# Dealing the stages of an RWKV-7 and feed-forward kernel so that each slot of a unit uses one TensorE tile mode

## The chip, the cores and the metric

The kernel runs on one core of one Trainium2 chip. The metric is the device time of the core in microseconds. Every number of a profile comes from one profiled execution of the program, whose own time is named beside its span.

## The reference

Two blocks, one after the other. The first is the RWKV-7 recurrence over batch 4, 8 heads, 768 steps, head dimension 40, in float32:

```
for t in range(S):
    y[:, :, t] = einsum('bhd,bhde->bhe', r_t, state)
    Sa = einsum('bhde,bhe->bhd', state, a_t)
    state = state * w_t[:, :, None, :] - einsum('bhd,bhe->bhde', Sa, b_t)
    state = state + einsum('bhd,bhe->bhde', v_t, k_t)
x = y.transpose(0, 2, 1, 3).reshape(B * S, H * D)      # 3072 tokens x 320
h = x @ w_in                                           # 320 -> 2048
out = (h * clip(h + 3, 0, 6) / 6) @ w_out              # 2048 -> 320
```

The two weight matrices come in double precision and the kernel converts them itself, early in the run.

## The kernel before

**Units.** The sequence is cut into 12 blocks of 64 steps. A unit is one block of two of the four batch entries, with all heads, so that its 2 x 64 rows fill the 128 partitions. There are 24 units, numbered 0 to 23, four to a group; unit 8 is the ninth. Units i and i+2 share a state tile, so the recurrence runs from unit i to unit i+2. Each unit goes through stages, each of which is a few TensorE instructions and then the evacuation of their result from PSUM by VectorE (DVE), ScalarE (ACT) or GpSimd (POOL):

- ahead of its turn (function `prepare`): W turned (transposed) and scanned into running products (`w_stage`, L584 and L604), gam and rgam made from them (`gam_stage`, second scan L615, copies L632 to L639), A, B and K turned and multiplied with them (L652, L660, L747), `factor` (rgam turned, copied to `rgt` at L722, and K and B scaled by it on POOL at L733 into `KBt`), F (64x64 products, four ACT copies L694 and L697, the matrix to be inverted), E (products, masked on DVE at L565) and EV (products, L766).
- in its turn (function `step`): RT and VT (R and V turned, L907 and L940), S (the state turned, L952 and L957), R (L929, L933), U (L979, L983), UT (L1022, L1028), C (products L539 in `scores`, masked on DVE at L565; then POOL copies V beside it at L1006 and SP fetches a later V at L470), rS (L1039, copied at L1045), H (L539, masked at L565), ysn (64 products L1082; its results go through DVE L1089 and POOL L1090 into `yg`, and into the state at L1094), and move and move2, eight DMAs of `yg` into the feed-forward input `xt` (L1130, L1135).

Every four units, a group's F is inverted by some 60 small DVE operations in turn (L812, L818; `invert`, in a list called `side`), and the first two units of the next group each carry a block of two small products (`third_block`, L848 and L872) that complete the inverse `tinv`, which U reads.

**Tile modes.** The page writes a matmul's stationary operand as rows*columns. The feed-forward products are 128*128. Turns from unit 8 on are 64*128 or 40*128 (two row halves, all columns). The recurrence's products are 64*64 or 40*64 (halves in both directions). I call these the full, the turn and the product mode.

**Slots and gaps.** From unit 8 on (the loop at the end of the kernel) each unit has five slots. A slot first issues the TensorE part of all its stages, and then all evacuations, in the order of the list `AFTER`. What a slot's stages write to PSUM lies in two tiles named `pair` of two banks each, of which there are two in all; the list `FILLS` says which stages share one. After each slot comes a gap of feed-forward pieces: 2.7 of them (2.2 in units 8 and 9; 3.6 while an inversion is in `side`, whose DVE steps are then laid between the pieces). A feed-forward job is half of a unit's hidden features, in eight pieces: four of `expand` (called e1 to e4; 8 instructions of 128x128 at L1186 each) and four of `contract` for the job before (L1227). A job also has 16 short 64*128 products on the third part of `xt` (`short`, kept in the list `narrow`). They are in the turn mode. Each slot begins by issuing them if they are waiting; otherwise they come out ahead of the third piece of `contract`. The first job of a unit can start once `xt` has landed.

The slots in the code, where the first number is the distance of the unit meant:

```
SLOTS = [
    [(0, "RT VT"), (-1, "U UT")],
    [(0, "S R"), (3, "EV"), (4, "E")],
    [(5, "A B"), (-1, "H")],
    [(6, "W"), (-1, "ysn"), (0, "C"), (6, "gam")],
    [(-1, "move move2"), (5, "K factor F"), (0, "rS")],
]
```

SP issues nearly all DMAs, in program order. In slots 3 and 4 its order is: W, V (after the POOL copy L1006), the eight of move and move2 (after `yg`), B and K of the next unit (after POOL's L733). Slot 0 adds R, slot 2 adds A, and the output rows (L1251) come after a unit's last contraction.

Of the kernel before, what the change touches and what calls it, by code (L numbers as in the profile page):

```python
# [12 lines left out]
ALU = mybir.AluOpType  # L13
# [5 lines left out]
BL = 64  # L19
# [12 lines left out]
def kernel(  # L32
# [42 lines left out]
    nc = tc.nc  # L75
# [373 lines left out]
    def fetch(name, i, engine=None):  # L449

        if i is None or i >= NK:
            return
        x, crossed = {"W": (w, 0), "A": (a, 0), "B": (b, 0), "K": (k, 0), "R": (r, 1),
                      "V": (v, 1)}[name]
        if name == "V":
            t = values[i % AHEAD if i < 2 * NU + AHEAD else (i - 2 * NU - 2) % NU]
        else:
            t = placed.get((name, i))
            if (name, i) == ("R", 1):
                t = others["K"]  # L460
            t = t if t is not None else (others if i < 2 * NU and i % 2 and name != "R" else inputs)[name]
        g, p = names[i]
        engines = engine or nc.sync
        for q in range(2):
            engine = engines[q] if isinstance(engines, tuple) else engines
            y = x[2 * p + q, :, g * BL:(g + 1) * BL, :]
            rows = slice(q * BL, (q + 1) * BL)
            if crossed:
                for s in range(2):
                    engine.dma_start(out=t[rows, 4 * s:4 * s + 4, 0:D],  # L470
                                     in_=y[s::2].rearrange("h t e -> t h e"))
# [57 lines left out]
    def half(i, n=SLOT):  # L529
        return slice(SLOT * i, SLOT * i + n)  # L530

    def scores(lhs, rhs, swap=False, placed=False):


        o = every_other(1) if placed else ps_pair(NPR, BL)
        for n in range(NPR):
            for q in range(2):
                for i in range(2):
                    nc.tensor.matmul(out=o[i][half(q), n ^ (2 * q * placed), :],  # L539
                                     lhsT=lhs[half(i, D), n ^ (2 * q * swap), half(q)],  # L540
                                     rhs=rhs[half(i, D), n, half(q)], start=True, stop=True)
        return o
# [26 lines left out]
    def prepare(i, F):  # L569
# [39 lines left out]
        def gam_stage():  # L609
# [5 lines left out]
            nc.vector.tensor_tensor_scan(out=back, data0=back, data1=start[:], initial=0.0,  # L615
                                         op0=ALU.mult, op1=ALU.add)
            nc.vector.memset(first, 1.0)
            if late and i % (NU + 3) == 0:
                gam = _ap(homes["prods1"][:], 0, [[P, NPR], [1, P]])
            else:  # L620
                gam = grp.tile([P, NPR, P], F32, name="gam", tag="gam", bufs=NU + 2)
# [84 lines left out]
        def factor_stage():  # L706

            if halves:
                wide = D if late else SLOT
                rg = ps_pair(NPR, wide)  # L710
                for pr in range(NPR):
                    for s in range(2):
                        nc.tensor.transpose(out=rg[s][:, pr, :], in_=o["rg"][half(s, wide), pr, :],
                                            identity=ident[half(s, wide), half(s, wide)])
            else:
                rg = ps_any([P, NPR, P])
                for pr in range(NPR):
                    nc.tensor.transpose(out=rg[:, pr, :], in_=o["rg"][:, pr, :], identity=ident[:])
            yield PE
            rgt = tmp.tile([P, H, D], F32, name="rgt", bufs=RGT)  # L720
            if halves:
                nc.scalar.activation(out=rgt[:].rearrange("p (r s) e -> p s r e", s=2), in_=rg[2][:, :, :, 0:D],  # L722
                                     func=AF.Copy)
            else:
                nc.scalar.activation(
                    out=rgt[:], in_=rg[:].rearrange("p r (s e) -> p (r s) e", s=2)[:, :, 0:D],
                    func=AF.Copy,
                )
            t = grp.tile([P, HD + WPAD], F32, name="KBt", tag="KBt", bufs=NU + 2)
            nc.gpsimd.memset(t[:, 2 * HD:], 0.0)  # L730
            for x, name in enumerate("KB"):
                o[name] = t[:, x * HD:x * HD + WPAD]
                nc.gpsimd.tensor_tensor(  # L733
                    out=o[name][:, 0:HD].rearrange("p (h e) -> p h e", h=H),
                    in0=o[name + "N"][:, :, 0:D], in1=rgt[:], op=ALU.mult,
                )
# [17 lines left out]
        def ev_stage():  # L754
# [10 lines left out]
            for x in range(2):  # L765
# [2 lines left out]
            o["EV"] = EV  # L768

        return {"W": w_stage, "gam": gam_stage, "A": a_stage, "B": b_stage, "F": f_by_32 if i < 2 * NU else f_by_64,  # L770
                "factor": factor_stage, "K": k_stage, "E": e_stage, "EV": ev_stage}

    def in_turn(stages, order):

# [118 lines left out]
    def step(i):  # L893
# [8 lines left out]
        def s_RT():  # L902
# [6 lines left out]
                fetch("R", i + 1)  # L909
            if fresh:  # L910
                nc.gpsimd.tensor_copy(last_dec[p][:], dec[:, 1])
                return
            scale = tmp.tile([P, 2, NPR], F32, name="scale", bufs=2)
            nc.gpsimd.tensor_tensor(out=scale[:], in0=last_dec[p][:], in1=dec[:, 0], op=ALU.mult)
            nc.gpsimd.tensor_copy(last_dec[p][:], dec[:, 1])
# [81 lines left out]
                                 func=AF.Copy, scale=-1.0)  # L997

        def s_C():
            x = scores(m["VT"], m["RT"])  # L1000
            yield PE
            if i < 2 * NU:
                m["K"] = masked(x)
                return
            masked(x, beside["K"][:, :, 0:BL])
            nc.gpsimd.tensor_copy(beside["K"][:, :, BL:JOIN].rearrange("p (r x) d -> p r x d", r=2),  # L1006
                                  VN[:].rearrange("p (x r) d -> p r x d", r=2)[:, :, :, 0:D])
            if i > 2 * NU:
                fetch("V", i + NU)

        def s_UT():

# [17 lines left out]

        def s_rS():

            ysp = [x.rearrange(("p (j q) t -> p j q t", "p r (j q) t -> p r j q t")[n // 2], q=2)
                   for n, x in enumerate(every_other(1))] if i >= 2 * NU else ps_pair(2, 2, BL)
            for j in range(2):
                for q in range(2):
                    for s in range(2):
# [7 lines left out]
            nc.scalar.activation(out=ys[:].rearrange("p (j r) q t -> p r j q t", r=2), in_=ysp[2], func=AF.Copy)  # L1045

        def s_sn():
            wide = SLOT if i < NU else D
# [84 lines left out]
        def s_move2():  # L1133
            for dst, src in m["moves"][4:]:
# [1 line left out]
            ready[i] = m["xt"]  # L1136
            yield from ()

        return {"RT": s_RT, "R": s_R, "VT": s_VT, "S": s_S, "U": s_U, "C": s_C, "UT": s_UT,
                "rS": s_rS,  # L1140
                "sn": s_sn, "ysn": s_ysn, "H": s_H, "y": s_y, "move": s_move, "move2": s_move2}

# [413 lines left out]


    SLOTS = [
        [(0, "RT VT"), (-1, "U UT")],
        [(0, "S R"), (3, "EV"), (4, "E")],  # L1560
        [(5, "A B"), (-1, "H")],
        [(6, "W"), (-1, "ysn"), (0, "C"), (6, "gam")],
        [(-1, "move move2"), (5, "K factor F"), (0, "rS")],
    ]
    FIRST_SLOTS = {
        (0, 0): [(0, "RT VT"), (5, "W"), (-1, "y"), (5, "gam")],
        (0, 1): [(-1, "move move2"), (0, "S R"), (4, "EV")],
        (0, 2): [(5, "A B")],
        (0, 3): [(6, "W"), (0, "C"), (6, "gam")],
        (0, 4): [(5, "K factor F"), (0, "rS")],  # L1570
        (1, 1): [(0, "S R"), (4, "E")],
    }
    FILLS = ["RT VT".split(), "U UT".split(), "S R EV".split(), ["E"], "A B".split(), ["H"],
             ["ysn"], "W C y".split(), "K factor".split(), "F rS".split()]
    AFTER = "U UT RT VT S EV R E H A B y ysn W C gam move move2 K factor F rS".split()
# [23 lines left out]
    def slot(i, j):  # L1599

        afresh()
        begun, taken = [], {}
        if narrow:
            narrow[0]()
        if j == 0 and i < NK:
            units[i] = step(i)
        for k, names_ in FIRST_SLOTS.get((i - 2 * NU, j), SLOTS[j]):
            u = i + k
            if u >= NK:
                continue  # L1610
            for name in names_.split():
                if k > 0 and u < 2 * NU + AHEAD and name != "EV":
                    continue
                if name == "W":
                    comings[u] = prepared(u)
                rest = (comings if k > 0 else units)[u][name]()
# [16 lines left out]

    begun_homes()
    begun_fixed()
    pairs.clear()
# [12 lines left out]
    while jobs or next(stream):  # L1649
        next(stream)  # L1650
# [30 lines left out]
```

## Time and profile before

| | |
|---|---|
| three runs | 818.2, 818.77, 815.56 us (median 818.2) |
| the profiled execution | 818.15 us, of which 816.4 us are the span from its first to its last instruction |
| PE (matmul) busy | 735.3 us, 90% of the span |
| PE weight loads | 617.7 us, 76% |
| DVE / ACT / POOL busy | 492.5 / 318.9 / 171.9 us |
| mean granted TensorE clock | 0.955 |
| the loop from unit 8 on | R turned for unit 8 at 312.9 us; last ysn at about 767 us |
| after the loop | feed-forward products alone, to about 805 us |

Of the page, the second part (40 slices of 20.4 us) shows PE at 9 tenths from the seventh slice on, and DVE between 2 and 8 tenths, high where an inversion runs. In the windows of the loop, DVE is busy for 26.0 of 29.0 us between 512 and 541 us (an inversion runs) and for 6.6 of 21.0 us between 711 and 732 us (none runs). A row of the timeline reads: start, duration, engine, line, operation, output and inputs, shape of the stationary operand (rows*columns), shape of the moving one, count. The ends of matmuls are modelled and overlap their successors, so what TensorE spends is read from start to start.

### The profile page before, as it was taken

Reading aid. Unit: us, or ns where it says so; the run is one execution under the profiler, and the core shown is the slowest. Engines: PE = TensorE matmul, PEld = TensorE weight load, DVE = VectorE, ACT = ScalarE, POOL = GpSimd, SP = SyncE. Lnnn points to the kernel's source line nnn. Section 1 sums busy time; section 2 is a strip of 40 time slices with the busy share of each in tenths; the row PEclk is TensorE's granted clock in tenths of the full one; section 3 lists DMA queues with packets and bytes.
Section 4 is the critical chain, followed back from the end, with each engine's and each line's share of the span. In section 5 each row is a group of like instructions: output and inputs, shape, how many; then the busy total and the mean of one; then the engine's idle time right before and its main releaser. Section 6 shows DMA issues by size and latency. Waiting matters only on the chain.

```text
span 816.4 us, 33518 instructions
## 1 busy us (share of the span) xinstructions
PE 735.3 (90%) x14960; PEld 617.7 (76%) x14960; DVE 492.5 (60%) x967; ACT 318.9 (39%) x646; POOL 171.9 (21%) x322
## 2 busy tenths in 40 slices
PE   5626768999999989999989999999999999999998
PEld 4626756878778877778778778878788887888886
DVE  7896786599545798445777355878344863232210
ACT  3348981323445333442333552333452234322121
POOL 6403002321222304222121222122022102110000
PEclk9855898999999999999989999999999999999999
DMA  9683554311233303231231222221211111100000
GB/s 122 119 188 104 140 134 76 67 27 26 54 63 58 67 20 58 49 62 29 54 58 29 45 44 50 55 54 35 51 41 31 21 35 29 25 15 19 20 9 17
DMA packets 174207, 44.91 MB, mean 55 GB/s; under 512 B 157424, under 2 KB 172784, under 8 KB 174064
## 3 DMA queue, kind: packets, MB, share of 16 engines
q1 hardware_dynamic: 169760, 42.03, 26.5%
q8 instruction: 118, 1.93, 1.0%
q10 hardware_dynamic: 4304, 0.74, 0.7%
q14 instruction: 25, 0.20, 0.1%
HBM read 34.08 MB, written 3.93 MB: 47 GB/s over the span
## 4 chain that ended last, share of the span: by engine, by line
PE 56%; DVE 24%; issue 6%; ACT 6%; SPq 4%; DMA 3%; POOL 2%; ACTq 0%; POOLq 0%; DVEq 0%
PE h L1186 18%; PE o L1227 11%; PE one L1227 7%; DVE x L818 4%; DVE prod L812 4%; PE pair L539 3%; PE pair L1082 2%; DVE prods L604 2%; DVE gt L1202 2%; SPq L473 2%; PE pair L499 2%; DVE area L565 2%; DVE area L615 2%; PE pair L929 1%; PE pair L1022 1%
## 5 line engine op out<-in xcount | busy, mean ns | idle before, releaser
L1186 PE MATMUL h<-xt,win 128*128 128x128 f32 (+1 forms) x2304 | 251.8, 283 | 4.8 <-DVE gt L1202 2.9
L1186 PEld LDWEIGHTS h<-xt,win 128*128 128x128 f32 (+1 forms) x2304 | 231.8, 192 | 20.0 <-DVE gt L1202 3.0
L1227 PE MATMUL o<-wout,gt 128*128 128x320 f32 x480 | 147.0, 448 | 0.0
L1202 DVE SCALAR_TENSOR_TENSOR gt<-gt,h 128x512 f32<-128x512 f32 x96 | 64.3, 684 | 136.2 <-ACT gt L1201 136.2
L1201 ACT ACTIVATE gt<-h,three 128x512 f32<-128x512 f32 x96 | 64.2, 687 | 156.4 <-PE h L1186 156.2
L1227 PEld LDWEIGHTS o<-wout,gt 128*128 128x128 f32 x480 | 87.0, 192 | 32.0 <-issue 1.2
L1227 PE MATMUL one<-wout,gt 128*128 128x320 f32 x288 | 88.5, 452 | 0.0
L1227 PEld LDWEIGHTS one<-wout,gt 128*128 128x128 f32 x288 | 53.4, 195 | 20.2 <-issue 1.6
L812 DVE TENSOR_TENSOR prod<-x 128x30 f32<-128x30 f32 (+9 forms) x180 | 63.1, 350 | 8.3 <-POOL x L797 3.3
L818 DVE TENSOR_TENSOR x<-x,prod 128x30 f32<-128x30 f32 (+9 forms) x180 | 62.1, 345 | 5.5
L1090 POOL TENSOR_TENSOR yg<-ys,gam 128x512 f32<-128x512 f32 x14 | 17.8, 1274 | 207.0 <-DVE ys L1089 129.4
L565 DVE COPY_PREDICATED area<-mask,pair 128x512 f32<-128x512 int32 x60 | 44.5, 746 | 20.3 <-PE pair L539 19.7
L604 DVE TENSOR_TENSOR_SCAN prods<-area,start 128x528 f32<-128x528 f32 x24 | 33.4, 1398 | 11.8 <-ACT area L595 10.3
L933 DVE TENSOR_TENSOR RR<-pair,EV 128x320 f32<-128x320 f32 x21 | 10.3, 490 | 48.1 <-ACT EV L766 29.8
L733 POOL TENSOR_TENSOR KBt<-K,rgt 128x320 f32<-128x320 f32 x22 | 19.0, 865 | 86.4 <-ACT rgt L722 66.2
L615 DVE TENSOR_TENSOR_SCAN area<-area,start 128x528 f32<-128x528 f32 x24 | 33.4, 1390 | 0.8
L834 POOL COPY tinv<-tb 32x1024 f32<-32x1024 f32 x10 | 10.3, 1035 | 84.9 <-DVE tb L821 84.6
L766 ACT ACTIVATE EV<-pair 64x320 f32<-64x320 f32 x44 | 18.8, 428 | 20.1 <-PE pair L761 17.4
L1082 PE MATMUL pair<-area,KBt 64*64 64x104 f32 x1024 | 26.6, 251 | 0.0
L636 POOL COPY gam<-prods 128x256 f32<-128x256 f32 x22 | 20.2, 916 | 29.8 <-DVE prods L604 29.7
L1082 PEld LDWEIGHTS pair<-area,KBt 64*64 64x64 f32 x1024 | 23.3, 132 | 2.1 <-issue 0.9
L722 ACT ACTIVATE rgt<-pair 128x320 f32<-128x320 f32 x16 | 7.0, 438 | 42.6 <-DVE kt L747 39.1
(300 smaller groups left out, 1113.3 us busy)
## 6 DMA issues: line engine op xcount, KB each, us to landing
V<-in_v_dram SPq DMA_DIRECT2D x96, 40.0 KB
out_dram<-ob SPq DMA_DIRECT2D x47, 80.0 KB
R<-in_r_dram SPq DMA_DIRECT2D x92, 40.0 KB
B<-in_b_dram SPq DMA_DIRECT2D x42, 80.0 KB
K<-in_k_dram SPq DMA_DIRECT2D x42, 80.0 KB
W<-in_w_dram SPq DMA_DIRECT2D x37, 80.0 KB
A<-in_a_dram SPq DMA_DIRECT2D x37, 80.0 KB
xt<-yg SPq DMA_DIRECT2D x72, 40.0 KB
```

The source lines that it names most:

```text
L539: nc.tensor.matmul(out=o[i][half(q), n ^ (2 * q * placed), :], lhsT=lhs[half(i, D), n ^ (2 * q * swap), half(q)], rhs=rhs[half(i, D), n, h ...
L565: nc.vector.copy_predicated(out=x[:].rearrange("p (i h) t -> p i h t", i=2), mask=mask8, data=o[2])
L604: nc.vector.tensor_tensor_scan(out=prods[:].rearrange("p r m i -> p (r m i)"), data0=wm[:, 0:SCAN], data1=start[:], initial=0.0, op0=ALU.m ...
L615: nc.vector.tensor_tensor_scan(out=back, data0=back, data1=start[:], initial=0.0, op0=ALU.mult, op1=ALU.add)
L636: nc.gpsimd.tensor_copy(gv[:, :, HB:BL], o["prods"][:, :, 1, 0:HB])
L812: nc.vector.tensor_tensor(out=pv, in0=_ap(x[:], (i + 1) * L + i, [[L, n], [0, i]]), in1=_ap(x[:], i * L, [[0, n], [1, i]]), op=ALU.mult,)
L818: nc.vector.tensor_tensor(out=rest, in0=rest, in1=pv, op=ALU.add)
L1082: nc.tensor.matmul(out=o2[q][half(s), pr, :], lhsT=o[name][half(q), h * D:h * D + SLOT], rhs=beside[name][half(q), 4 * rs + 2 * (s ^ (q * ...
L1186: nc.tensor.matmul(out=hp[c][:, i, :], lhsT=lhsT, rhs=rhs, start=(begun[c] == 0), stop=(begun[c] == 3 * NQ - 1))
L1201: nc.scalar.activation(out=gt[:], in_=hp[c][:], func=AF.Relu, bias=three[:], scale=1.0)
L1202: nc.vector.scalar_tensor_tensor(out=gt[:], in0=gt[:], scalar=6.0, in1=hp[c][:], op0=ALU.min, op1=ALU.mult)
L1227: nc.tensor.matmul(out=op[:], lhsT=gts[c][:, n, :], rhs=wout[:, c * HJ + r * NQ + n, :], start=((split or r == 0) and c == 0 and n == 0), ...
```

## The change

The same stages are done for the same units, dealt anew over the five slots from unit 8 on:

- Slots 0 and 2 have turns only (RT VT W S; A B K factor). Slots 1, 3 and 4 have products only (EV R H; ysn C F; U UT E rS).
- W and gam come for the unit five ahead, not six; S goes from slot 1 to 0; K and `factor` from slot 4 to 2; F from 4 to 3; U and UT from slot 0 of the next unit to slot 4 of the same one; H of the unit before from slot 2 to 1; E from slot 1 (four ahead) to slot 4 (five ahead); EV from three to four ahead.
- The scaling of K and B by `rgt` (POOL, L733) becomes a stage of its own, KB, in slot 3, and with it the fetches of the next B and K. The decay of the state (POOL L914, DVE L916) becomes a stage `scale`, in slot 4 of the unit before.
- V keeps five buffers throughout, and the fetch in C is for the unit five ahead, not four.
- The short feed-forward products wait in slots 1 and 4 for the next slot of turns, if enough pieces are left before they are due.
- The blocks of the inverse run in the gaps after slots 2 and 3, not 3 and 4. The first of these loops' units has a list of its own: y of unit 7 goes from slot 0 to 1, and its move and move2 from slot 1 to 2.

```diff
-            t = values[i % AHEAD if i < 2 * NU + AHEAD else (i - 2 * NU - 2) % NU]
+            t = values[i % AHEAD]
...
-    def scores(lhs, rhs, swap=False, placed=False):
+    def scores(lhs, rhs, swap=False, placed=False, apart=False):
-        o = every_other(1) if placed else ps_pair(NPR, BL)
+        o = every_other(1) if apart else ps_pair(NPR, BL)
...
-            if late and i % (NU + 3) == 0:
+            if late and i % (NU + 3) == NU + 2:
...
+            o["rgt"] = rgt
+            if not late:
+                scaled_kb()
+
+        def kb_stage():
+            scaled_kb()
+            yield from ()
+
+        def scaled_kb():
+
             t = grp.tile([P, HD + WPAD], F32, name="KBt", tag="KBt", bufs=NU + 2)
...
-                return
+            elif i < 2 * NU:
+                decay()
+
+        def s_scale():
+            decay()
+            yield from ()
...
-            x = scores(m["VT"], m["RT"])
+            x = scores(m["VT"], m["RT"], apart=i >= 2 * NU)
...
-            if i > 2 * NU:
-                fetch("V", i + NU)
+            fetch("V", i + AHEAD)
...
-            ysp = [x.rearrange(...)
-                   for n, x in enumerate(every_other(1))] if i >= 2 * NU else ps_pair(2, 2, BL)
+            ysp = ps_pair(2, 2, BL)
...
     SLOTS = [
-        [(0, "RT VT"), (-1, "U UT")],
-        [(0, "S R"), (3, "EV"), (4, "E")],
-        [(5, "A B"), (-1, "H")],
-        [(6, "W"), (-1, "ysn"), (0, "C"), (6, "gam")],
-        [(-1, "move move2"), (5, "K factor F"), (0, "rS")],
+        [(0, "RT VT"), (5, "W"), (0, "S"), (5, "gam")],
+        [(4, "EV"), (0, "R"), (-1, "H")],
+        [(5, "A B K factor")],
+        [(-1, "ysn"), (0, "C"), (5, "F KB")],
+        [(-1, "move move2"), (0, "U UT"), (5, "E"), (0, "rS"), (1, "scale")],
     ]
...
+    FIRST_SLOTS = [
+        SLOTS[0],
+        [(4, "EV"), (0, "R"), (-1, "y")],
+        [(-1, "move move2"), (5, "A B K factor")],
+        [(0, "C"), (5, "F KB")],
+        [(0, "U UT"), (5, "E"), (0, "rS"), (1, "scale")],
+    ]
+    FILLS = ["RT VT".split(), "W S".split(), "R EV".split(), "H y".split(), "A B".split(), "K factor".split(),
+             ["ysn"], "C F".split(), "U UT".split(), "E rS".split()]
+    AFTER = "RT VT W S gam EV H y R A B K factor F ysn C KB move move2 U UT E rS scale".split()
+    TURNS_NEXT, LEFT = (1, 4), {"e1": 5, "e2": 4, "e3": 3, "e4": 2, True: 1}
...
-        if narrow:
+        if narrow and (j not in TURNS_NEXT or LEFT[place[0]] < pieces_due[0] + NORMAL):
             narrow[0]()
...
-            if i % NU == 0 and j == 3 and i < NK:
+            if i % NU == 0 and j == 2 and i < NK:
                 aside(3 * L)
                 blocks[i], blocks[i + 1] = third_blocks()
...
-                (lambda: run(blocks[i])) if i < NK and i % NU < 2 and j > 2 else None)
+                (lambda: run(blocks[i])) if i < NK and i % NU < 2 and j in (2, 3) else None)
```

More of the change, by code (lines that the diff above doesn't have):

```diff
@@ L734, in factor_stage @@
                     out=o[name][:, 0:HD].rearrange("p (h e) -> p h e", h=H),
-                    in0=o[name + "N"][:, :, 0:D], in1=rgt[:], op=ALU.mult,
+                    in0=o[name + "N"][:, :, 0:D], in1=o["rgt"][:], op=ALU.mult,
                 )
@@ L770, in prepare @@
         return {"W": w_stage, "gam": gam_stage, "A": a_stage, "B": b_stage, "F": f_by_32 if i < 2 * NU else f_by_64,
-                "factor": factor_stage, "K": k_stage, "E": e_stage, "EV": ev_stage}
+                "factor": factor_stage, "KB": kb_stage, "K": k_stage, "E": e_stage, "EV": ev_stage}
     def in_turn(stages, order):
@@ L911, in s_RT, with decay @@
                 nc.gpsimd.tensor_copy(last_dec[p][:], dec[:, 1])
-                return
+            elif i < 2 * NU:
[3 more added lines that the diff above has]
+            yield from ()
+        def decay():
             scale = tmp.tile([P, 2, NPR], F32, name="scale", bufs=2)
@@ L1031, in s_rS @@
         def s_rS():
-            ysp = [x.rearrange(("p (j q) t -> p j q t", "p r (j q) t -> p r j q t")[n // 2], q=2)
-                   for n, x in enumerate(every_other(1))] if i >= 2 * NU else ps_pair(2, 2, BL)
+            ysp = ps_pair(2, 2, BL)
             for j in range(2):
@@ L1044, in s_rS @@
             ys = m["ys"] = tmp.tile([P, NPR, 2, BL], F32, name="ys", tag="yg", bufs=2)
-            nc.scalar.activation(out=ys[:].rearrange("p (j r) q t -> p r j q t", r=2), in_=ysp[2], func=AF.Copy)
+            nc.scalar.activation(out=ys[:].rearrange("p (j r) q t -> p r j (q t)", r=2),
+                                 in_=ysp[2].rearrange("p r j q t -> p r j (q t)"), func=AF.Copy)
         def s_sn():
@@ L1137, in s_move2 @@
             yield from ()
-        return {"RT": s_RT, "R": s_R, "VT": s_VT, "S": s_S, "U": s_U, "C": s_C, "UT": s_UT,
+        return {"RT": s_RT, "scale": s_scale, "R": s_R, "VT": s_VT, "S": s_S, "U": s_U, "C": s_C, "UT": s_UT,
                 "rS": s_rS,
@@ L1558 @@
     SLOTS = [
-        [(0, "RT VT"), (-1, "U UT")],
-        [(0, "S R"), (3, "EV"), (4, "E")],
-        [(5, "A B"), (-1, "H")],
-        [(6, "W"), (-1, "ysn"), (0, "C"), (6, "gam")],
-        [(-1, "move move2"), (5, "K factor F"), (0, "rS")],
-    ]
[L1565 to L1575, printed above, removed]
+        [(0, "RT VT"), (5, "W"), (0, "S"), (5, "gam")],
[3 more added lines that the diff above has]
+        [(-1, "move move2"), (0, "U UT"), (5, "E"), (0, "rS"), (1, "scale")],
+    ]
+    FIRST_SLOTS = [
[8 more added lines that the diff above has]
+    AFTER = "RT VT W S gam EV H y R A B K factor F ysn C KB move move2 U UT E rS scale".split()
     NORMAL, DENSE, STEPS_OF = 2.7, 3.6, 2.2
+    TURNS_NEXT, LEFT = (1, 4), {"e1": 5, "e2": 4, "e3": 3, "e4": 2, True: 1}
     steps_due, pieces_due = [0.0], [0.0]
@@ L1602, in slot @@
         begun, taken = [], {}
-        if narrow:
+        if narrow and (j not in TURNS_NEXT or LEFT[place[0]] < pieces_due[0] + NORMAL):
             narrow[0]()
-        if j == 0 and i < NK:
-            units[i] = step(i)
-        for k, names_ in FIRST_SLOTS.get((i - 2 * NU, j), SLOTS[j]):
+        for k, names_ in (FIRST_SLOTS if i == 2 * NU else SLOTS)[j]:
             u = i + k
@@ L1611, in slot @@
             for name in names_.split():
-                if k > 0 and u < 2 * NU + AHEAD and name != "EV":
+                if k == 5 and u < 2 * NU + AHEAD:
                     continue
@@ L1615, in slot @@
                     comings[u] = prepared(u)
-                rest = (comings if k > 0 else units)[u][name]()
+                if name == "scale":
+                    units[u] = step(u)
+                rest = (comings if k > 0 and name != "scale" else units)[u][name]()
                 fill = [n for n, x in enumerate(FILLS) if name in x]
@@ L1635 @@
     begun_fixed()
+    units[2 * NU] = step(2 * NU)
+    for _ in units[2 * NU]["scale"]():
+        pass
     pairs.clear()
```

## The prediction

> **What bounds the kernel now.** I read the page first, then the waits of PE in the loop that the change rewrites (312 to 768 us), the timeline from start to start, the windows for the clock, and SP's queue. The page says that TensorE sets the end:
>
> ```profile
> span 816.4 us, 33518 instructions
> PE 735.3 (90%) x14960; PEld 617.7 (76%) x14960; DVE 492.5 (60%) x967; ACT 318.9 (39%) x646; POOL 171.9 (21%) x322
> PE   5626768999999989999989999999999999999998
> ```
>
> From the seventh slice on PE is at 9 tenths nearly throughout, and after the loop 38 us of feed-forward work are left (767 to 805 us). So the end comes when PE has done its work: what the loop saves on PE, in matmul starts or in waits, comes off the end, as long as the feed-forward always has a unit to work on. The waits in the loop:
>
> ```profile
> engine line waited for: us in total, times, longest us
> PE pair L979 <- ACT ys L1045: 3.5, 2, 1.8
> PE pair L872 <- ACT rgt L722: 1.9, 2, 0.9
> PE pair L848 <- DVE state L1094: 1.9, 5, 0.9
> PE pair L979 <- issue: 1.5, 2, 1.3
> PE h L1186 <- DMA xt<-yg: 1.3, 1, 1.3
> ```
>
> All rows together are 16.1 us, and no one of them comes in every unit. Next, what a change of tile mode costs. The timeline of one turn slot, around its last turn:
>
> ```profile
> 523.80 0.41 PE L499 MATMUL pair<-ident,A 64*128 64x64 f32 x8
> 524.04 0.43 PE L499 MATMUL pair<-ident,B 64*128 64x64 f32 x8
> ...
> 524.24 0.22 PE L499 MATMUL pair<-ident,B 64*128 64x64 f32 x1
> 524.39 0.69 PE L539 MATMUL pair<-RT,UT 40*64 40x64 f32 x32
> 525.02 0.38 PE L1186 MATMUL h<-xt,win 128*128 128x128 f32 x1
> ```
>
> The last turn of A starts at 523.99 and the first of B at 524.04: 0.05 to 0.06 us within the mode. The last turn of B starts at 524.24 and the first product at 524.39: 0.15. So the switch costs 0.093. In the same way: last product to feed-forward 0.148 (524.87 to 525.02) against 0.038 from product group to product group, 0.110 more; feed-forward to turn or to product 0.205 behind L1186 and 0.363 behind L1227, against 0.112 and 0.270 within the mode, 0.093 more; short product to any other mode 0.201 against 0.105, 0.096. These gaps repeat to 0.002 us all over the loop.
>
> **Part one, the switches.** In the trace's loop I count 71 switches from feed-forward to turns or short products, 71 from these to products, 82 from products to feed-forward, 11 from feed-forward straight to products and one from turns to feed-forward: 236. That is what the slots give: 63 slots with turns and products (3 each), 19 with products alone (2 each, and 8 of them have short products ahead, one more), one with turns alone. Their cost is 154 x 0.093 + 82 x 0.110 = 23.3 us. For the new slots I walked the loop piece by piece: 27 turn slots and 50 product slots are left (slot 2 is empty from unit 19 on). Of the 31 issues of short products, 19 join a turn slot and cost no switch, 6 stand ahead of a product slot, and 6 stand alone where slot 0 or 2 is empty. So 77 + 6 entries, 6 from short products to products, 33 exits from the turn mode, 50 from the product mode: 172 switches, 122 x 0.093 + 50 x 0.110 = 16.8 us. **Saved: 6.5 us**; at most 8 if no short product stood badly, at least 0 where PE would have waited anyway.
> The Trainium skill, page "TensorEngine Tiling (Array Packing)", section Key Properties, says that a change of the tiling mode, not of the tile alone, drains the TensorE, and the page "TensorE: Matmul & The Clock Gate", Part 2, puts a drain at about 128 cycles of the array. At the 2.4 GHz it names that is an estimate of 53 ns, and 64 switches would be 3.4 us, so that the sum below would come out 3.1 us higher; the rows here show about twice as much a switch, and they decide.
>
> **Part two, the waits that go.** U stands in slot 0 today, and its `pair` tile is that of F and rS of slot 4. How that waits:
>
> ```profile
> 540.23 0.69 DVE L747 TENSOR_TENSOR kt<-pair,rgam 128x512 f32<-128x512 f32 x1
> ...
> 540.95 0.44 ACT L722 ACTIVATE rgt<-pair 128x320 f32<-128x320 f32 x1 [6.45 <-DVE kt L747]
> ...
> 543.26 0.60 ACT L1045 ACTIVATE ys<-pair 128x512 f32<-128x512 f32 x1
> ...
> 543.91 0.68 PE L979 MATMUL pair<-RR,tinv 64*64 64x40 f32 x32 [1.74 <-ACT ys L1045]
> ```
>
> K's product is late on DVE, behind slot 3's two scans and the inversion's steps; `rgt` shares K's tile and waits for it (so 11 times of 11, 39.1 us of ACT's idle time); four copies of F and ys follow, and only then may U write. And the clock falls behind such a wait:
>
> ```profile
> 541.50:545.00 3.50, 1.76 (x82) 1.56 (x81) 0.53 (x1) 3.44 (x7) 2.00 (x4) 0.99 0.16 48
> 545.00:548.40 3.40, 3.40 (x13) 2.20 (x8) 3.23 (x9) 1.92 (x5) 0.00 (x0) 0.50 0.21 42
> ```
>
> (duration, then PE to POOL, then the granted clock.) 0.50 for 3.4 us here and for 6.8 us from 422.1, behind waits of 0.92 and 1.75: 5.1 us of work lost. In the new order U's tile was ysn's, and slot 4 has three ACT copies instead of six. So U's 3.5 and 1.5, R's waits for `rgt` and ys (0.9 and 0.4) and the 5.1 go: **-11.4 us**. What is late next is DVE behind slot 0, where W's two scans and gam now stand: from the slot's start 2.65 us of ACT copies, 4.1 us of DVE (1.59 + 0.24 + 1.47 + 0.07 + 0.29 + 0.48), 1.4 for two feed-forward results, 2.7 for eight inversion steps of 0.34, R's sum 0.49 and H's mask 0.76 end at 12.1, while slot 2 starts at 10.5 and asks for R's tile at once and for H's half a us later. That is 1 us in the units in which an inversion or its end lies there (11, 12, 15, 16): **+3.5** (0 to 5). Without inversion the same sum ends 2.7 earlier, and slot 2 is not held.
>
> **Part three, blocks and first unit.** The waits of the blocks (1.9, 1.9, 0.6, 0.5) and of U for `tinv` (0.6) are 5.5 today. Then the first block product follows A and B instead of ysn; behind the inversion's two transposes (2 us each on DVE) it will wait some 0.9 in units 12 and 16, and U comes some 0.35 us before `tinv` is copied in six units: 3.9, **-1.6**. In unit 8 A waits behind gam and R's sum, 1.7 instead of the 0.9 of today; the 0.8 of L687 behind a scan goes: 0.
>
> **Part four, xt.** This is the added cost. B and K are fetched in slot 3 now, so in SP's queue they stand ahead of move; V too, and it waits for the POOL copy behind C's mask. SP today:
>
> ```profile
> 414.22 2.57 SPq L470 DMA_DIRECT2D V<-in_v_dram  x4
> 416.84 3.11 SPq L1130 DMA_DIRECT2D xt<-yg  x4
> ```
>
> ysn of that slot began at 407.4, so V was issued 6.8 and the fourth DMA of move 11.9 us behind it. After: ysn, C and F 2.6; F's four copies 1.92; C's mask, which shares F's tile and so waits as `rgt` does, 0.76; the copy 0.46; V 2.57; B and K 2.8; to the fourth DMA 2.4: 13.7 with the steps between. It lands 2.4 (unit 9, used without wait) to 3.3 us later (unit 7, waited for): 16.1 to 17.0. The first feed-forward product of units 8 and 11 comes 13.4 us behind ysn if nothing waits: slot 3 2.7, five pieces 5.0, a block 0.7, slot 4 2.15, entries and exits 0.5, slot 0 1.15, a last piece 1.17; that of unit 10 at 13.6 with 0.5 more of DVE delay on the chain. Units 9 and 14 need it at 16.5, units 12, 13 and later a slot later. I take 2.5 us for each of the three, near the low end since U's wait for `tinv` moves two of them back, and half clock behind two of them at 2.2 (between 1.7 and 3.4): 7.5 + 4.4, less the 1.3 and 0.7 that xt's products wait today: **+9.9** (-2 to +27).
>
> **Sum.** -6.5 - 11.4 + 3.5 - 1.6 + 9.9 = -6.1, from the profiled execution's 818.15 us (span 816.4 and 1.75 around it), which is the median of the runs to 0.05: **812.0 us**.
>
> **Rivals.**
> - xt is in time: if C's mask doesn't wait for F, V and all behind it come 1.3 us earlier, and other waits in those slots push the products back the rest. Then the 11.9 aren't paid: 800. For it: move leads by 7 to 10 us in most units today. Against it: unit 9 has 2.4 and is just not held.
> - Nothing is gained, the change doesn't do what it says: where inversions run, DVE is busy for 26.0 of 29.0 us (512 to 541), and the switches saved there return as waits; if the -11.4 comes back too behind slot 0's scans, 818 (815 to 822).
> - Slower: SP's queue sets the pace. V took 3.4 and 3.7 us to issue in two units instead of 2.57, and with that and the late landing xt is 1.7 us later than I took it: three waits of 4.2, two of 1.2 (units 9 and 14), three long half-clock stretches of 3.4 and one short of 1.7 are 27 instead of 11.9: 826. It decides from 22 us of such waits on, which is 822.
>
> **Chances.** Forecast 0.42 (807 to 815), xt in time 0.23 (797 to 806), no gain 0.17, slower 0.18 (822 to 832). 0.5%, 4.1 us, is about what can be told from no change: faster by more than that (below 814.1) 0.60, within it 0.22, slower 0.18. The range of 8 in 10 is 799 to 824.
>
> **What would show it.** Switches: no gap of 0.15 between a turn and a product behind it, 172 switches in the loop. Part two: L979 no longer in PE's waits behind ys; L499 or L713 behind RR or a mask instead. Part four: h L1186 behind xt in units 8, 10 and 11, and a granted clock of 0.5 behind it. I am wrong if h waits for xt nowhere or in most units, or if one wait comes in every unit.

## The result and the profile after

Over 20 runs each, the changed kernel takes 820.88 us (815.12 to 824.74) and the kernel before 815.6 us (808.72 to 819.61): a ratio of 1.0068, 95% interval 1.0043 to 1.0094. It is 5 us slower where I forecast 6 us faster; the number lies inside the range, on the other side of no change.

The page of the profiled execution after (817.8 us with a span of 816.1):

```profile
span 816.1 us, 33536 instructions
PE 728.8 (89%) x14960; PEld 614.8 (75%) x14960; DVE 487.4 (60%) x967; ACT 318.2 (39%) x646; POOL 172.3 (21%) x322
PE   5626769999999998999998889998999999999998
```

PE does the same 14960 matmuls in 6.5 us less busy time, and yet the span is the same: more slices stand at 8 tenths. The two profiled executions hardly differ, since that of before lies 2.5 us above the median of its 20 runs and that of after 3.1 us below: it had a mean clock of 0.958, while its 20 runs have 0.953. The comparison of times is therefore that of the runs; the profiles tell what the time consists of.

The waits of PE in the loop, to be read against the rows of before (16.1 us in all); a last row of 0.2 is left out:

```profile
engine line waited for: us in total, times, longest us
PE h L1203 <- DMA xt<-yg: 7.4, 3, 3.6
PE pair L1055 <- issue: 4.7, 4, 1.6
PE pair L858 <- DVE bt L660: 4.4, 4, 1.4
PE pair L970 <- DVE state L934: 2.8, 1, 2.8
PE pair L882 <- issue: 1.9, 3, 0.8
PE h L1203 <- DVE start L613: 1.5, 1, 1.5
PE pair L997 <- DVE state L1111: 1.1, 1, 1.1
```

U (now L997) no longer waits for `ys`, as forecast. In place of that stand the first feed-forward product behind `xt` (L1203; its row behind `start` is the same wait, for it ends 1.36 us behind the issue of the last of move's four DMAs, and the three others end 1.30 us behind theirs), the two block products (L858, L882), S of unit 8 (L970), and rows that I had not thought of: rS (L1055) and the second block product waiting for "issue", that is, for nothing that the profile shows. All rows together, with two stops of 0.13 us that are too short for this view, are 24.4 us.

**A ledger of the loop.** From R of unit 8 to the last ysn the loop takes 453.9 us before and 455.1 after; what follows is 49.6 in both. I take three things from each trace: the loop's length, PE's waits of over 0.1 us in it, and half of every stretch in which the clock was granted at 0.50. The remainder is PE's work with its switches. Ratios and medians are of the runs, the other columns of the one profiled execution:

| kernel | median us | ratio to before, 95% | loop | waits | half clock | remainder |
|---|---|---|---|---|---|---|
| before | 815.6 | | 453.9 | 16.1 | 5.1 | 432.7 |
| changed | 820.88 | 1.0068 (1.0043, 1.0094) | 455.1 | 24.4 | 5.1 | 425.6 |
| `bk_behind_move` | 808.42 | 0.990 (0.985, 0.995) | 445.4 | 17.0 | 3.4 | 425.0 |
| `e_in_slot_1` | 825.14 | 1.011 (1.006, 1.015) | 460.0 | 24.2 | 11.9 | 423.9 |
| `k_first` | 817.94 | 1.003 (0.999, 1.006) | 453.1 | 21.1 | 6.8 | 425.2 |
| `e_four_times` | 834.17, one run | | 469.0 | 24.6 | 11.9 | 432.5 |
| `bk_and_e` | 807.48 | 0.991 (0.988, 0.994) | 443.8 | 14.5 | 3.4 | 425.9 |
| `all_four` | 805.61 | 0.988 (0.983, 0.993) | 441.3 | 11.9 | 3.4 | 426.0 |
| `all_four_s_between` | 805.87 | 0.989 (0.985, 0.994) | 443.0 | 11.5 | 1.7 | 429.8 |
| `before_bk_ahead` | 845.47 | 1.036 (1.031, 1.042) | 479.5 | 28.5 | 17.1 | 433.9 |
| `all_five` | 803.75 | 0.983 (0.980, 0.987) | 437.8 | 10.9 | 0 | 426.9 |
| `all_six` | 801.95 | 0.980 (0.977, 0.984) | 434.5 | 8.1 | 0 | 426.4 |
| `five_s_between` | 807.31 | 0.987 (0.984, 0.991) | 442.7 | 11.4 | 1.7 | 429.6 |

Where a wait lies within a half-clock stretch, half of it is counted twice and the remainder is that much too small: 0.3 us in the kernel before, 1.8 in `before_bk_ahead`, at most 0.2 elsewhere.

The last column settles half of the question: it is 7.1 us lower after the change, and it stays within 3 us in every kernel that has the new slots and neither work nor switches added. The switches were saved. The question is what filled the column of waits.

**Where PE stops for "issue".** Slot 4 of a unit with a block, in the timeline of after:

```profile
576.45 0.65 PE L539 MATMUL pair<-at,kt 40*64 40x64 f32 x32
576.91 0.45 PE L1055 MATMUL pair<-RT,S 40*64 40x64 f32 x17
578.46 0.46 PE L1055 MATMUL pair<-RT,S 40*64 40x64 f32 x15 [1.09 <-issue]
```

The stop falls inside one group of 32 equal products, after the 17th, where no operand or buffer can be late. I counted the instructions of PE's queue from the start of the trace (matmuls, weight loads, and the semaphore instructions among them): all nine stops of after (6.9 us), and one of before (0.48), come at number 193 or 194 of a run of 256, and 1.29 to 1.53 us behind the end of a packet of the queue that carries instructions:

```profile
q8 instruction: 118, 1.93, 1.0%
```

118 packets of 16 KB for PE's 29920 matmuls and weight loads and the 311 other instructions of its queue are one to every 256. In the loop two of these packets never start less than 3.3 us apart, while slot 4's groups (U, UT, E, rS) use 256 instructions in some 2 us, and a block product just ahead of them 128 more in 0.7. So where these groups come together PE runs out of instructions. The change brought them together: E and U moved into slot 4, the second block into the gap ahead of it.

**Theory and rivals.** Theory: `xt` is late behind B and K, as part four says, and the supply of instructions, which I had not seen, takes what the switches gave. First rival: the supply is all, and `xt` would wait little without it. Second rival: the switches are worth little, because PE waits for DVE in their place.

### The profile page after: what moved, and what is told of

The parts are those of the page before. It is cut to its first block, busy times and chain, and to the rows that moved or that the text cites. A ratio compares the mean times of both kernels' runs of the same rounds, so it can differ in the third digit from the quotient of the medians.

```text
span 816.1 us, 33536 instructions
## 1 busy us (share of the span) xinstructions
PE 728.8 (89%) x14960; PEld 614.8 (75%) x14960; DVE 487.4 (60%) x967; ACT 318.2 (39%) x646; POOL 172.3 (21%) x322
## 4 chain that ended last, share of the span: by engine, by line
PE 62%; DVE 16%; issue 7%; SPq 5%; ACT 4%; DMA 3%; POOL 1%; ACTq 0%; POOLq 0%; DVEq 0%
PE h L1203 23%; PE o L1244 11%; PE one L1244 7%; DVE prod L822 4%; DVE x L828 4%; PE pair L539 3%; PE pair L1099 3%; SPq L473 3%; PE pair L499 2%; DVE gt L1219 2%; SPq L470 1%; DVE area L565 1%; PE pair L771 1%; PE pair L947 1%; PE pair L997 1%
## 5 line engine op out<-in xcount | busy, mean ns | idle before, releaser
L1203 PE MATMUL h<-xt,win 128*128 128x128 f32 (+1 forms) x2304 | 254.9, 286 | 10.4 <-DMA xt<-yg 7.4
L1203 PEld LDWEIGHTS h<-xt,win 128*128 128x128 f32 (+1 forms) x2304 | 234.2, 195 | 28.3 <-issue 10.5
L1244 PE MATMUL one<-wout,gt 128*128 128x320 f32 x288 | 85.1, 442 | 0.0
L822 DVE TENSOR_TENSOR prod<-x 128x30 f32<-128x30 f32 (+9 forms) x180 | 64.8, 360 | 8.4 <-POOL x L807 3.4
L1244 PEld LDWEIGHTS one<-wout,gt 128*128 128x128 f32 x288 | 52.3, 190 | 19.4
L604 DVE TENSOR_TENSOR_SCAN prods<-area,start 128x528 f32<-128x528 f32 x24 | 30.1, 1259 | 27.1 <-ACT area L584 17.0
L636 POOL COPY gam<-prods 128x256 f32<-128x256 f32 x22 | 12.4, 563 | 108.4 <-DVE prods L604 108.3
L615 DVE TENSOR_TENSOR_SCAN area<-area,start 128x528 f32<-128x528 f32 x24 | 31.2, 1300 | 0.8
L1106 DVE TENSOR_TENSOR ys<-pair,ys 128x512 f32<-128x512 f32 x16 | 11.1, 691 | 27.9 <-PE pair L1099 27.9
L1099 PE MATMUL pair<-area,KBt 64*64 64x104 f32 x1024 | 27.2, 252 | 0.3
L694 ACT ACTIVATE F<-pair 32x256 f32<-32x256 f32 x32 | 11.9, 373 | 34.1 <-PE pair L687 33.9
L637 POOL COPY rgam<-prods 128x256 f32<-128x256 f32 x22 | 24.5, 1114 | 0.0
```

The source lines that it names most:

```text
L604: nc.vector.tensor_tensor_scan(out=prods[:].rearrange("p r m i -> p (r m i)"), data0=wm[:, 0:SCAN], data1=start[:], initial=0.0, op0=ALU.m ...
L637: nc.gpsimd.tensor_copy(rv[:, :, 0:HB], o["prods"][:, :, 0, 0:HB][:, :, ::-1])
L822: nc.vector.tensor_tensor(out=pv, in0=_ap(x[:], (i + 1) * L + i, [[L, n], [0, i]]), in1=_ap(x[:], i * L, [[0, n], [1, i]]), op=ALU.mult,)
L1099: nc.tensor.matmul(out=o2[q][half(s), pr, :], lhsT=o[name][half(q), h * D:h * D + SLOT], rhs=beside[name][half(q), 4 * rs + 2 * (s ^ (q * ...
L1203: nc.tensor.matmul(out=hp[c][:, i, :], lhsT=lhsT, rhs=rhs, start=(begun[c] == 0), stop=(begun[c] == 3 * NQ - 1))
L1244: nc.tensor.matmul(out=op[:], lhsT=gts[c][:, n, :], rhs=wout[:, c * HJ + r * NQ + n, :], start=((split or r == 0) and c == 0 and n == 0), ...
```

## The experiments

**B and K behind move.** Their fetches become a stage of their own, issued in slot 4 behind move2:

```diff
+            if not late:
+                fetch_bk()
+
+        def fetch_bk():
             for name in "BK":
                 fetch(name, following(i))
...
-        [(-1, "move move2"), (0, "U UT"), (5, "E"), (0, "rS"), (1, "scale")],
+        [(-1, "move move2"), (0, "U UT"), (5, "E BK"), (0, "rS"), (1, "scale")],
```

> The changed kernel with one edit: the fetches of the next B and K go out behind move and move2 in slot 4, no longer ahead of them in slot 3. Theory 1 (xt late behind B and K in SP's queue): move is issued 2.8 us earlier, so the waits of h for xt in units 8, 9, 10 and 14 (1.9, 1.5, 3.6 and 1.9 us in the trace of the changed kernel, 8.9 in sum) fall to under 2 us in sum, and two of its three half-clock stretches of 3.4 us go with them (1.7 us of work each): 8 to 10 us faster than the changed kernel, so 5 us or more faster than the one before. Theory 2 (the loss is in the PE's instruction supply and in the other waits): xt's waits go but the time moves by under 3 us, as what was late behind them waits elsewhere.

0.990 of before, against 1.0068: 0.0168 of 815.6, so 13.7 us in the runs (the two intervals lie apart), 9.7 in the loop of the profiled executions. First SP and the product that waits for it in the changed kernel, for `xt` of unit 10 (ysn began at 414.26):

```profile
420.24 3.52 SPq L470 DMA_DIRECT2D V<-in_v_dram  x4
423.87 1.29 SPq L473 DMA_DIRECT2D B<-in_b_dram  x2
425.25 1.28 SPq L473 DMA_DIRECT2D K<-in_k_dram  x2
426.58 3.13 SPq L1147 DMA_DIRECT2D xt<-yg  x4
...
431.01 1.36 PE L1203 MATMUL h<-xt,win 128*128 128x128 f32 x7 [3.62 <-DMA xt<-yg]
```

B and K hold move up by 2.7 us. Then PE's waits in this experiment:

```profile
PE pair L866 <- DVE bt L660: 5.7, 4, 2.4
PE pair L1063 <- issue: 4.6, 4, 1.6
...
PE h L1211 <- DMA xt<-yg: 0.6, 1, 0.6
```

8.9 us of waits for `xt` have become 0.6. The stops for "issue" are still there (6.3 in all): the first rival has fallen.

**E back in slot 1.** E goes from slot 4 to slot 1 (four units ahead, as before the change), and EV to three ahead; B and K stay ahead of move:

```diff
-        [(4, "EV"), (0, "R"), (-1, "H")],
+        [(3, "EV"), (0, "R"), (-1, "H"), (4, "E")],
...
-        [(-1, "move move2"), (0, "U UT"), (5, "E"), (0, "rS"), (1, "scale")],
+        [(-1, "move move2"), (0, "U UT"), (0, "rS"), (1, "scale")],
```

> The changed kernel with one edit: the products of E go back to slot 1 (for the unit four ahead, EV three ahead), so slot 4 has three product groups and slot 1 four. Theory 1 (instruction supply): in the changed kernel TensorE stops in the middle of a group, without any semaphore, always at the same place of a block of 256 instructions and 1.3 to 1.5 us behind the end of an instruction fetch; nine such stops, 6.9 us, all in units with a block product next to slot 4's 256 instructions. With 64 instructions fewer there the stops at L1055 (4.7 us) go or fall below 1 us: 3 to 5 us faster than the changed kernel. Theory 2 (the stops are rS waiting for data): they stay as they are, and the time with them.

The stops are gone but for 0.2, so they do come from E's place; and the kernel is not faster. In the runs it has 1.011 of before against 1.0068, with intervals that overlap; the loop of its profiled execution is 4.9 us longer:

```profile
PE h L1203 <- DMA xt<-yg: 13.0, 4, 4.0
...
PE pair L539 <- issue: 0.2, 1, 0.2
```

```profile
368.40:378.60 10.20, 10.08 (x157) 9.77 (x158) 2.14 (x5) 0.86 (x2) 0.23 (x2) 0.50 0.23 43
```

(The second fence is a window; the last three figures are the clock, the DMA share and GB/s.) Without the stops the feed-forward product comes earlier, while `xt` comes as late behind ysn as before (only in unit 8 it is 1.3 us earlier): 14.9 us of waits for it in place of 8.9, in units 8 to 11 and 14, with 20.5 us of half clock behind three of them. In the changed kernel the stops had hidden part of the delay of `xt`; 4.3 of the 6 us more are in units 8 and 11, the rest fits the time of E itself (0.49 us a unit), which is now spent ahead of ysn. In unit 11 stops of 0.51 and 1.58 stand between ysn and the product, which then waits for nothing; here it waits 2.96. So the two costs don't add up: taking the stops away is worth nothing while `xt` is late.

**K first.** K and its factor are turned ahead of A and B, in both slot lists and in `AFTER`:

```diff
-        [(5, "A B K factor")],
+        [(5, "K factor A B")],
```

> The changed kernel with one edit: slot 2 has the order K, factor, A, B instead of A, B, K, factor, on TensorE and behind it. The first block product L858 follows in the tile of whichever comes first. Theory 1 (it waits for B's product on DVE): its waits (1.4, 1.1, 1.1, 0.7 us in units 12, 13, 16, 17, 4.4 in sum) fall by half or more as K is one DVE operation and B is the second of two: 2 us faster than the changed kernel. Theory 2 (DVE's queue as a whole is late there): the wait moves to ysn or to another tile of slot 3 and the time stays within 1 us.

The first block product (L858), which writes to a tile that A and B had, waits 3.4 us, now behind `rgt`, in place of 4.4 behind B's product. The ratio's interval (0.999 to 1.006) holds both 1 and the changed kernel's 1.0068: this can't be told from no change.

**E four times.** In units without a block, E's products are issued four times into the same tile. If the stops come from the rate of instructions, they must appear where there were none:

```diff
+            for _ in range(3 if late and (i - NU - 1) % NU > 1 else 0):
+                for n in range(NPR):
+                    ...
+                            nc.tensor.matmul(out=x[j][half(q), n, :], lhsT=o["kt"][half(j, D), n, half(q)],
```

> The changed kernel, but E's products in slot 4 are issued four times into the same place where the unit has no block (units 10, 11, 14, 15, 18), so that 448 small instructions stand in a row there. Plain cost: 3 x 0.49 us in five units, 7.4 us. Theory 1 (instruction supply): stops in the middle of a product group without a semaphore appear in these units too, 0.5 to 2 us each, 5 us or so in sum beside the 6.9 that are there. Theory 2 (the stops belong to the blocks or to data): no such stop appears in these five units.

```profile
427.43 1.46 PE L765 MATMUL pair<-at,kt 40*64 40x64 f32 x86
430.16 0.38 PE L765 MATMUL pair<-at,kt 40*64 40x64 f32 x9 [1.26 <-issue]
```

They do: 1.40, 1.26, 1.35 and 1.28 us in four of the five units that got the products, and again at number 193 or 194 of 256. Here 86 products stand ahead of the stop, not 17: the place is set by the count, not by the group. Of the changed kernel's own 6.9 us of stops 2.9 are left here, so that all are 8.1: those of units 12 and 13 are gone, where the added instructions have moved the count. Half clock follows two of these four stops, for 3.4 us each. The ledger puts the 480 added products at 6.9 us (432.5 against 425.6) and the added half clock at 6.8.

**Both, and then four.** `bk_and_e` joins the first two edits. `all_four` adds `k_first`, and the decay of unit 8's state goes ahead of the two clearings on POOL that S of unit 8 had waited behind:

```diff
-    begun_homes()
-    begun_fixed()
     units[2 * NU] = step(2 * NU)
     for _ in units[2 * NU]["scale"]():
         pass
+    begun_homes()
+    begun_fixed()
```

> Both edits at once: the fetches of B and K behind move, and E in slot 1. Theory 1 (xt late and the instruction supply are two causes that hid each other: with E in slot 1 alone TensorE reached xt 4 us sooner and waited there): both kinds of wait are gone, under 1.5 us in the loop for each, and the kernel is 4 to 6 us faster than with the fetches alone, about 803 us beside 814.7 of the kernel before. Theory 2 (with the stops gone xt is late again, also behind move): h waits for xt for 4 us or more, and the time stays at 808.

> The two edits, K and factor ahead of A and B, and the decay for unit 8 issued ahead of the two memsets that begin the loop. Theory 1: S of unit 8 waits 1.8 us instead of 2.85, and its half-clock stretch may go; L858's waits fall from 5.7 to about 3.5: 2 to 4 us faster than with B, K and E alone, about 800 us. Theory 2: the freed time returns as other waits (xt, or DVE's masks), and the time is that of the two edits within 1 us.

With `xt` in time, E in slot 1 takes 4.2 us of stops away and the loop is 1.6 us shorter; the runs show no difference (0.991 against 0.990). 1.7 came back as small waits, for K's fetch (0.7) among others. `all_four` is 2.5 us shorter in the loop than `bk_and_e`; the intervals overlap.

**The price of the switches.** S goes from slot 0 (turns) to slot 1, between EV and R, in all units: a turn between products again. 32 switches more than in `all_four` were expected; the traces have 28 (199 against 171, without the blocks of the inverse), since in the four units without EV the turn opens the slot and costs one switch.

```diff
-        [(0, "RT VT"), (5, "W"), (0, "S"), (5, "gam")],
-        [(3, "EV"), (0, "R"), (-1, "H"), (4, "E")],
+        [(0, "RT VT"), (5, "W"), (5, "gam")],
+        [(3, "EV"), (0, "S R"), (-1, "H"), (4, "E")],
```

> As the one with all four edits, but S, eight turns, stands in slot 1 between the products of EV and R, where it costs two changes of tile mode in each of 16 units. Theory 1 (a change of mode costs 0.093 to 0.110 us and PE's time is the kernel's): 32 more changes, 3.2 us slower than all four edits. Theory 2 (the loop has slack that takes it): within 1 us. In the trace the starts show 0.15 from the last product of EV to the first turn of S and from the last turn to R either way.

The medians differ by 0.3 us, which by itself speaks for the second rival. The ledger says why not: the remainder rose by 3.8, while S of unit 8 lost its wait of 1.8 and the 1.7 of half clock behind it. The edit had mended something else. So I moved S of unit 8 alone in `all_five`, and compared again in `five_s_between`:

```diff
     FIRST_SLOTS = [
-        SLOTS[0],
-        [(4, "EV"), (0, "R"), (-1, "y")],
+        [(0, "RT VT"), (5, "W"), (5, "gam")],
+        [(4, "EV"), (0, "S R"), (-1, "y")],
```

> All four edits at once and a fifth: in unit 8, the first of the loop, S goes from slot 0 to slot 1, between EV and R, so that it no longer waits for the decayed state at the start of the loop. With all four edits that wait was 1.8 us and the clock was at half for 3.4 us from 316.8, 1.7 us of work lost. If both are real costs of TensorE: 3.5 us off the span of 803.7, less one switch of mode more (0.2), so 800.4. If only the wait moves to another place of unit 8 (R or A behind the same decay), the span stays within 1 us of 803.7.

> The five edits, with S in slot 1 (between EV and R) in all units, not in unit 8 alone. This puts a turn between products in 15 more units: 30 switches of mode more, 15 of 0.093 and 15 of 0.110 by the prices of the prediction, 3.0 us. If a switch costs what the start-to-start gaps say and TensorE has no slack in this loop: 3.0 us above the five edits. If what the switches save is waited for elsewhere: within 1 us of them.

The two ran beside each other: 803.75 and 807.31 us, 3.56 us (the means differ by 3.3, give or take 2.8). 30 switches at 3.0 us were expected; the traces have 26 (199 against 173), which are 2.6 us at the prediction's prices, and the remainder rose by 2.7. The rest of the loop's 4.9 us is 0.5 of waits and a half-clock stretch. The second rival has fallen, and a switch costs about 0.1 us here. `all_five` itself is 3.5 us shorter in the loop than `all_four` (the span only 1.7, not the 3.3 expected, since its loop began 1.8 later).

**The block later.** `all_six` issues the first block product ahead of the last piece of the gap after slot 2, not in its middle:

```diff
-            if between and k == n // 2:
+            if between and k == (n - 1 if last else n // 2):
...
+                j == 2)
```

> The five edits and a sixth: the first block product (zp) is issued ahead of the last piece of the gap after slot 2, not in the middle of it, so that it stands one to two pieces (1.2 to 2.4 us) later behind A and B. With all four edits zp waited 1.09, 0.90 and 1.88 us in units 12, 13 and 16, and the clock was at half for 3.4 us behind the last. If those waits are lost work: 3.5 us less of waits and 1.7 of half clock, so 5 us below the five edits. If the whole chain behind zp (its copy, the second product, tinv, U) only moves back by the same amount, U waits for tinv instead and the two kernels are equal within 1 us.

```profile
PE pair L866 <- ACT rgt L722: 2.4, 4, 1.1
PE pair L539 <- issue: 1.8, 3, 1.0
PE h L1211 <- DMA xt<-yg: 1.6, 2, 1.2
PE pair L499 <- DMA K<-in_k_dram: 0.7, 2, 0.4
```

The block's wait falls from 4.6 to 2.4 us, the medians by 1.8, the loop by 3.3; U does not wait for `tinv` in its place. 5 were expected, of which 1.7 were a half clock that was gone already. Its profiled execution, 796.82 us, is the fastest of its six, so the median and the ratio count: 0.980 (0.977 to 0.984) of before, and the lowest median of all versions here.

**The kernel before, with B and K ahead of move.** Part four on the old slots: in `AFTER` of before, K and `factor` go ahead of move and move2, and with them the two fetches.

```diff
-    AFTER = "U UT RT VT S EV R E H A B y ysn W C gam move move2 K factor F rS".split()
+    AFTER = "U UT RT VT S EV R E H A B y ysn W C gam K factor move move2 F rS".split()
```

> The kernel before the change with one edit: in slot 4 the stages K and factor, and so the fetches of the next B and K, stand ahead of move and move2 in the order of evacuation. Theory 1 (xt late behind B and K is a cause by itself, without any new slot order): h waits for xt in units 7 to 14, 6 us or more in sum instead of 1.9, and the time rises by 5 to 10 us. Theory 2 (xt was late in the changed kernel because its products come sooner): the waits stay under 3 us and the time within 2 us.

845.47 us, 27.2 more in the span than before: far more than expected. Waits rose by 12.4 us and the loss at half clock by 12.0. The waits for `xt` alone are 15.3. But this edit does more than put two fetches ahead. They wait for POOL, which scales K and B (L733) with `rgt` behind K's product, and SP issues in order:

```profile
352.12 3.47 SPq L470 DMA_DIRECT2D V<-in_v_dram  x4
361.37 0.86 POOL L733 TENSOR_TENSOR KBt<-B,rgt 128x320 f32<-128x320 f32 x1
362.26 1.27 SPq L473 DMA_DIRECT2D B<-in_b_dram  x2
364.97 3.12 SPq L1130 DMA_DIRECT2D xt<-yg  x4
```

In this unit SP stands still for 6.7 us between V and B, in unit 10 for 5.2, in six others for 0.8 to 2.7, ahead of the 2.7 us of the fetches themselves. In the changed kernel B follows V within 0.1 us. So the run shows what a late `xt` costs, but it is no clean measure of the two fetches; that is `bk_behind_move`. Nor does each late `xt` draw a half clock: of the four stretches three stand behind waits for `xt`, and one behind U's wait for `ys`, with the next wait for `xt` (2.85 us) inside it:

```profile
438.80:449.00 10.20, 7.35 (x28) 6.05 (x28) 6.45 (x20) 1.91 (x4) 0.00 (x0) 0.50 0.30 59
```

I had sized neither SP's standing still nor the half clock of 6.8 to 10.2 us that some of the waits draw. How long such a stretch becomes is the part of `xt`'s price that I could not forecast.

## Why the prediction was wrong, by its steps

**Part one, the switches (-6.5): right.** Counted as the 236 were, 171 switches are left (forecast 172), which are 6.6 us less at the prediction's prices; the remainder fell by 7.1; 26 switches put back added 2.7 to it, and 3.56 us in the runs.

**Part two (-11.4 and +3.5): what goes went, DVE was over-sized.** U's waits for `ys`, R's for `rgt` and `ys`, and the half clock behind them are gone. DVE behind slot 0's scans holds nothing in slot 2; the one wait for DVE of this kind is U's 1.1 behind the state's sum. 2.4 better than forecast.

**Part three (-1.6): too small.** The blocks wait 4.6 us, nearly all of it in four units, where I had 1.8 in two, and 2.1 of U for `tinv` that does not occur. In unit 8 I named A as what would wait. It was S, 2.84 us behind the decay, for which POOL is kept by a copy of `tinv` (2.13 us) and two clearings (0.52 each); 1.7 of half clock follow. 3.5 worse than forecast in all.

**Part four (+9.9): right in size by luck, and not in place.** Forecast were 7.5 of waits in units 8, 10 and 11 and 4.4 of half clock. The trace has 8.9 in units 8 (1.89), 9 (1.52), 10 (3.62) and 14 (1.85), and 3.4 of half clock behind the waits at 370 and 431: 12.3 against 11.9. Unit 9 was held because V took 3.2 us to issue there, not 2.57, and because two stores of output rows (1.2 us, L1268) stand between K and move; my chain had no term for them. `xt` came 17.75 us after ysn where I had 16.1 to 17.0. In unit 14, the other one that I did not expect, the same stores stand there (1.2 us). Unit 11 was not held, because of the stops ahead of it. The size holds only beside these stops, which were not in the forecast: in `e_in_slot_1`, without them, `xt` cost 14.9 of waits and 10.2 of half clock, 25.2 in place of 11.9. Moving the two fetches brought 13.7 us in the runs.

**What was not in the sum: the supply of instructions.** The step that failed is the first one, that what the loop saves "in matmul starts or in waits, comes off the end", with a list of waits that held only what engines and DMAs owe each other. I priced each group at its own rate and never asked whether PE would be given 384 small instructions within 5 us, although before had one stop of this kind (0.48 us). It is 6.9 us in the changed kernel, more than the whole gain I forecast. With the other misses: -0.6 (the remainder, 7.1 in place of 6.5), -2.4 (DVE), +3.5 (blocks and unit 8), +6.9 (stops), +0.4 (`xt`), and -0.6 of a small wait of before that is gone are +7.2, and -6.1 becomes +1.1; the loop grew by 1.2. This is an account of where the time stood, not of what mending one term would bring: without the stops `xt` takes their place, and with `xt` in time they cost little. Ahead of the loop the profiled execution was 1.5 us faster, hence the equal spans. The runs say 5.3. That the other runs lose more at half clock than the profiled one fits their lower mean clock (0.005 of 816 us is 4.1), but where they lose it no trace shows.

**The rivals.** `xt` in time was worked out to 800; with B and K behind move the kernel takes 808.42, short by the stops and the blocks. "No gain" came near in number (818), but its reason, DVE, is not what the trace shows, and the number is not that of its own conditions: 812.0 with the 6.5 of the switches back is 818.5, and with the 11.4 back in place of the 3.5 it is 826.4. The slower case had the place right and needed 27 us of waits and half clock from `xt` (which on 812.0 is 827, not 826); there were 12.3 beside the stops, and 25.2 without them, where the kernel takes 825.14. None of my cases held the stops. Parts one to three without part four were -16.0. `all_six`, with the late fetches, most of the stops, unit 8's S and half of the blocks' wait mended, is 0.0197 of 815.6, 16.1 us, below before. That the two numbers agree is partly luck, since its edits also mend waits that part one to three did not count on (its loop is 19.4 us shorter); but the parts were sound, and the order in two queues and one slot ate them.

**What stays open.** Why the runs lose 5.3 us where the loops of the two profiled executions differ by 1.2. The stops' own price: beside a late `xt` they cost nothing on balance, without it 4.2 us less of them gave 1.6 in the loop. And which waits draw a half clock: 1.89 us at 370.0 did, 1.85 at 555.0 did not, nor did 2.15 in `all_five`.

## What to carry over

When stages are dealt anew, walk every queue that an instruction passes: a DMA queue in program order first (two fetches of 1.3 us each ahead of the transfer that feeds the bounding engine cost 14 us), and with each entry what it waits for itself, since a queue in order holds all behind it (6.7 us in one unit of `before_bk_ahead`). Walk TensorE's own instructions too, and count how many small ones come in a row. Waits on one engine are no sum: one can hide another, and mending the visible one first may show the other in full. A ledger of length, waits and half clock, kept for each kernel, tells work from waiting when the medians can't.

## What the runs showed of the hardware

- TensorE can run out of instructions. With 40- and 64-wide products at about 14 ns each, weight load included, it stopped for 0.1 to 1.6 us at a fixed place (number 193 or 194) of every 256 instructions, 1.2 to 1.6 us behind the end of a 16 KB instruction packet; these packets started at least 3.3 us apart. The Trainium skill, page "Runtime: NRT & Kernel Launch", section "Instruction fetch mechanics", says that instructions come in blocks of 256 and that crossing a block is mostly hidden. The blocks agree with this trace; the hiding does not hold where groups of such products follow each other.
- The half clock came in stretches of 3.4, 6.8 or 10.2 us behind waits of 0.9 to 4.0 us, also behind stops for instructions (396.4 and 430.5 us in `e_four_times`), but not behind all. In the worst kernel (`before_bk_ahead`) it cost 17.1 us beside 28.5 of waits, 1.8 of which are counted in both.
